# Moving the last two second-stage pieces of one batch two steps ahead in a hand-written schedule

## The chip, the cores and the metric

The kernel runs on one core of one Trainium2 chip. The metric is the time of one execution on the device in microseconds (us). A core has a matrix engine (PE, whose weight loads are listed as PEld), a vector engine (DVE), a scalar engine (ACT), a general engine (POOL) and a queue engine (SP), which run side by side and wait for each other through semaphores. SP and POOL issue the transfers (DMA).

## The reference

The input x has 8 batches of 3008 tokens with 256 channels. Each batch is filtered along the token axis by a Fourier transform, a multiplication with a complex filter and the inverse transform. The result goes, token by token, through a layer pair with a leaky activation whose slope is given per hidden unit:

```python
X = np.fft.rfft(x, axis=1)                  # x: 8 x 3008 x 256
Y = X * (filt_r + 1j * filt_i)[None]
y = np.fft.irfft(Y, n=3008, axis=1).reshape(24064, 256)
h = y @ w_in                                # 256 x 2048
g = np.maximum(h, 0) + alpha * np.minimum(h, 0)
out = g @ w_out                             # 2048 x 256
```

## The kernel before

The transform of 3008 = 47 x 64 points is done in stages of matrix products. For each batch there are four kinds of pieces. Sixteen `piece_a` are the 47-point transform: a matmul (L245) into a psF bank, evicted to `asb` by ACT (L324), saved to `a_dram` and read back turned as `at`. Twelve `piece_b`, numbered by `kp`, are the **second stage**: two matmuls (L265) each and an eviction by ACT (L269) into one of six slots of `uw_s`. Twelve `piece_c` are the first step back (matmuls L292, evicted by ACT to `v`, L324); `turn_c` writes a quarter of `v` to `v_dram` after each third of them (L301), and after the last `load_z` reads it back as `zt` (L310). Sixteen `piece_d` end it (matmuls L317, evictions to `yT`, L324).

Between the second stage and `piece_c` the filter is applied, for two pieces at a time, by `scale`:

```python
if kp % 2:
    late.append((self.scale, (kp, iu - 1)))
...
uu, ww = w[:, 512 * iu : 512 * iu + 1024], w[:, 0:1024]
...
nc.vector.tensor_mul(...[:, 0 : iu // 2 + 1 : iu // 2], uu..., f)     # L278
for o in (0, 64):
    nc.gpsimd.dma_start(out=uu[o : o + 64], in_=ww[64 - o : 128 - o], accum_op=OP.add)   # L281
```

One DVE multiply (L278) makes both products of a pair. One stays in the pair's own slots (`uu`), the other goes to slots 0 and 1 of `uw_s` (`ww`), which all pairs share. Two transfers issued by POOL (L281) then add `ww`, with its halves of the partitions swapped, to `uu`. `piece_c` reads `uu` after that.

The layer pair runs over 47 blocks of 512 tokens, each of 16 steps, so there are 752 steps in all; step 16n + j does row group j of block n. `up` makes the two matmuls of a step (L618) into `hps`; on every second step ACT evicts two row groups to `gtb` (L634), and DVE makes the negative part times slope minus one in `m_s` (two L640; in row group 6 ACT makes it, L638). After every fourth step the sum of the two is owed, and `settle` does it on DVE (L821) in the step that follows. The second layer follows about a block behind, so many matmuls per step, either as plain products (`eight`, L669) or with fewer products of sums (`seven`, L691). Blocks 3 and 4 are of the second kind. Their sums on DVE (L650, L652, L658) are placed by the table `SUMS`: for block 3 from step 65 on. `seven` begins with 16 matmuls over the rows of the block in order, and goes on to the products with the sums in `ss`.

The order of all work is written out by hand. `PLACES` gives, for each batch after the first, the steps of the pieces a, b, c and d. `put` files them, and each step runs in this order: what is in `late` from the step before, the sums, the pieces of this step, `settle`, `up`, and the matmuls of the second layer:

```python
flush()
for b, w, h in ahead.pop(step, ()): ...
    b.sums(w, h)
for fn, args in plan.pop(step, ()):
    fn(*args)
settle()
blk.up(j)
while todo and done < (step - LAG) / 16: ...
```

An engine's instructions stand in the order in which the program writes them. In batch two the second-stage pieces 8 and 9 stand on step 58 and are scaled on step 59; pieces 10 and 11 stand on steps 63 and 64 and are scaled on step 65; the last `piece_c` stand on steps 70 to 72, `turn_c` on 72 and 73, and the first `piece_d` on step 80.

Of the kernel before, what the change touches and what calls it, by code (L numbers as in the profile page):

```python
# [20 lines left out]
NH = 32  # L21
PLACES = (
    ((3, 4, 4, 6, 14, 15, 17, 17, 19, 19, 22, 22, 24, 24, 25, 25),
     (34, 34, 38, 38, 45, 46, 52, 52, 58, 58, 63, 64),
     (48, 50, 55, 55, 55, 60, 66, 70, 71, 71, 72, 72),
     (80, 80, 80, 80, 82, 89, 92, 95, 100, 101, 103, 107, 109, 118, 124, 150)),
    ((-34, -32, -31, -29, -27, -21, -21, -20, -18, -18, -17, -16, -12, -11, -10, -10),
# [857 lines left out]
```

## Time and profile before

| what | value |
|---|---|
| median of 3 runs | 761.42 us |
| the runs | 761.05, 761.42, 762.9 us |
| the profiled execution | 762.9 us |
| its span | 761.1 us |
| granted clock of PE | 0.999 |
| mean DMA rate | 142 GB/s |

The profile is of one execution. Times in its rows count from the start of its span; about 1.8 us of the execution lie around the span. A row of a timeline gives the start, the length from the first start to the last end, the engine, the line, the operation with its tiles, and in brackets how long the engine stood idle before it and what ended that. Lengths of neighbouring rows overlap, since an operation's length takes in its way through the engine; what one costs in a row of them is seen from start to start. Names of tiles stand without their buffer numbers.

### The profile page before, as it was taken

The numbers are of one execution on the slowest core, as the hardware profiler recorded it, in microseconds if no ns is written. First come the engines' busy times: TensorE is split into PE (matmuls) and PEld (weight loads), VectorE is DVE, ScalarE is ACT, GpSimd is POOL, SyncE is SP. The second block draws the span as 40 slices with busy tenths as digits, with TensorE's granted clock in tenths as the row PEclk, the third lists the DMA queues.
The fourth block names the chain that finished last, engine by engine and source line by source line (L and its number), as shares of the span: only waits on it lengthen the run. The fifth ranks groups of instructions, "written<-read, shape, count | busy, mean of one in ns | idle before, by whom it ended". The sixth has DMA issues, their size and how long they took to land.

```text
span 761.1 us, 19855 instructions
## 1 busy us (share of the span) xinstructions
PE 744.2 (98%) x7812; PEld 539.6 (71%) x7812; DVE 694.6 (91%) x1298; ACT 673.8 (89%) x1083; POOL 162.4 (21%) x236
## 2 busy tenths in 40 slices
PE   7989989999999999999999999999999999999998
PEld 5746656776777777776778777777677776777766
DVE  5887877998999998899999999999998998999994
ACT  6898989999999998999899998999989898888873
POOL 9631421132021220232013211221100221010100
PEclk9999999999999999999999999999999999999999
DMA  9995888868975597666876659865586355522122
GB/s 163 192 233 154 146 163 227 181 139 169 197 160 126 110 186 180 139 126 135 192 166 142 134 120 198 184 139 114 106 184 137 74 108 112 140 61 67 43 65 62
DMA packets 100790, 107.97 MB, mean 142 GB/s; under 512 B 10568, under 2 KB 81496, under 8 KB 100696
## 3 DMA queue, kind: packets, MB, share of 16 engines
q1 hardware_dynamic: 80136, 70.05, 35.9%
q0 software_dynamic: 20416, 36.58, 29.9%
q8 instruction: 61, 1.00, 0.6%
q14 instruction: 33, 0.27, 0.1%
q10 hardware_dynamic: 144, 0.07, 0.0%
HBM read 55.41 MB, written 46.66 MB: 134 GB/s over the span
## 4 chain that ended last, share of the span: by engine, by line
PE 90%; DVE 3%; DMA 3%; ACT 1%; issue 1%; SPq 0%; POOL 0%; DVEq 0%; ACTq 0%
PE hps L618 40%; PE op L691 30%; PE op L669 6%; PE psF L245 3%; PE psF L317 3%; PE psF L265 2%; PE psF L292 2%; DMA uw_s<-uw_s 2%; DVE gtb L821 1%; DVE m_s L640 1%; PE op L723 1%; ACT gtb L634 1%; PE hps L364 1%; DVE uw_s L278 1%; DMA zt<-v_dram 1%
## 5 line engine op out<-in xcount | busy, mean ns | idle before, releaser
L618 PE MATMUL hps<-yT,win_s 128*128 128x512 f16 (+3 forms) x1600 | 447.4, 366 | 0.4 <-ACT yT L324 0.4
L634 ACT ACTIVATE gtb<-hps 128x1024 f16<-128x1024 f32 x376 | 386.1, 1028 | 51.3 <-PE hps L618 48.5
L691 PEld LDWEIGHTS <-gtb 128*128 128x128 f16 x3040 | 206.0, 98 | 100.0 <-issue 1.0
L640 DVE TENSOR_SCALAR m_s<-gtb,alm_s 128x512 f16<-128x512 f16 x705 | 215.3, 351 | 35.5 <-ACT gtb L634 34.0
L821 DVE TENSOR_TENSOR gtb<-gtb,m_s 128x2048 f16<-128x2048 f16 x188 | 229.3, 1220 | 5.3 <-ACT m_s L638 3.2
L618 PEld LDWEIGHTS <-win_s 128*128 128x128 f16 x1600 | 135.2, 98 | 25.5 <-issue 3.9
L691 PE MATMUL op<-wout_s,gtb 128*128 128x128 f16 x1824 | 153.2, 219 | 0.0
L281 POOL DMA_DIRECT2D uw_s<-uw_s x84 | 72.3, 1002 | 332.5 <-DVE uw_s L278 207.7
L691 PEld LDWEIGHTS <-ss 128*128 128x128 f16 x1216 | 83.1, 98 | 39.1 <-DVE ss L652 1.6
L691 PE MATMUL op<-tw_s,gtb 128*128 128x128 f16 x1216 | 105.0, 219 | 0.0
L691 PE MATMUL op<-tw_s,ss 128*128 128x128 f16 x1216 | 103.6, 219 | 1.3 <-DVE ss L652 1.3
L669 PE MATMUL op<-wout_s,gtb 128*128 128x256 f16 x512 | 76.9, 272 | 0.3 <-DVE osb L594 0.3
L656 POOL DMA_DIRECT2D gtb<-gtb x28 | 28.0, 998 | 207.5 <-ACT gtb L634 139.1
L669 PEld LDWEIGHTS <-gtb 128*128 128x128 f16 x512 | 50.0, 98 | 31.3
L324 ACT ACTIVATE asb<-psF 96x512 f16<-96x512 f32 x112 | 65.7, 601 | 1.8 <-PE psF L245 0.9
L324 ACT ACTIVATE yT<-psF 128x376 f16<-128x376 f32 x118 | 56.8, 493 | 4.7 <-PE psF L317 3.7
L278 DVE TENSOR_TENSOR uw_s<-uw_s,filt 128x2048 f16<-128x2048 f16 x42 | 51.2, 1220 | 5.7 <-DMA uw_s<-uw_s 4.0
L324 ACT ACTIVATE v<-psF 128x512 f16<-128x512 f32 x88 | 52.0, 603 | 5.1 <-PE psF L292 4.1
L201 POOL DMA_DIRECT2D xs<-in_x_dram x64 | 52.0, 977 | 5.2 <-issue 2.4
L269 ACT ACTIVATE uw_s<-psF 128x512 f16<-128x512 f32 x84 | 50.0, 605 | 2.9 <-PE psF L265 2.0
L652 DVE TENSOR_TENSOR ss<-ss,gtb 128x1024 f16<-128x1024 f16 x76 | 52.0, 685 | 0.1
L650 DVE TENSOR_TENSOR ss<-gtb 128x1024 f16<-128x1024 f16 (+1 forms) x75 | 51.9, 692 | 0.0
(125 smaller groups left out, 643.1 us busy)
## 6 DMA issues: line engine op xcount, KB each, us to landing
out_dram<-osb SPq DMA_DIRECT2D x127, 128.0 KB
xs<-in_x_dram POOLq DMA_DIRECT2D x64, 188.0 KB, 5.5
a_dram<-asb SPq DMA_DIRECT2D x28, 384.0 KB
uw_s<-uw_s POOLq DMA_DIRECT2D x84, 128.0 KB, 3.4
v_dram<-v SPq DMA_DIRECT2D x112, 96.0 KB
zt<-v_dram SPq DMA_DIRECT2D x28, 384.0 KB
at<-a_dram SPq DMA_DIRECT2D x20, 384.0 KB
gtb<-gtb POOLq DMA_DIRECT2D x28, 256.0 KB, 3.8
```

Of the source, the lines that this page charges most:

```text
L201: nc.gpsimd.dma_start(out=xc[(b, c)][h * N1 : h * N1 + N1], in_=xrow(b, h, c))
L278: nc.vector.tensor_mul(w.rearrange("p (i d) -> p i d", d=1024)[:, 0 : iu // 2 + 1 : iu // 2], uu.unsqueeze(1).to_broadcast([128, 2, 1024]), f)
L281: nc.gpsimd.dma_start(out=uu[o : o + 64], in_=ww[64 - o : 128 - o], accum_op=OP.add)
L324: nc.scalar.activation(o, i, AF.Copy)
L618: nc.tensor.matmul(self.hps[:, j % 2, ca:cb], win_s[:, kt, j * 128 : (j + 1) * 128], yT[:, kt, at : at + cb - ca], start=(kt == 0), stop=( ...
L634: nc.scalar.activation(g, hs, AF.Copy)
L640: nc.vector.tensor_scalar(ms[:, i], g[:, i], 0.0, a, OP.min, OP.mult)
L650: nc.vector.tensor_add(z1, a21, a22)
L652: nc.vector.tensor_add(z2, z1, a11)
L669: nc.tensor.matmul(op[:, si % 2], self.pair(k // 2)[:, k % 2, 128 * si : 128 * si + 128], wout_s[:, k], start=(k == 0), stop=(k == 15))
L691: nc.tensor.matmul(acc[:, 128 * i : 128 * i + 128], x[:, k, 128 * i : 128 * i + 128], b[:, k], start=first and k + i == 0, stop=k == 7, sk ...
L821: nc.vector.tensor_add(g, g, ms)
```

## The change

The last two second-stage pieces of batch two, `kp` 10 and 11, stand on steps 61 and 62 instead of 63 and 64.

```diff
 PLACES = (
     ((3, 4, 4, 6, 14, 15, 17, 17, 19, 19, 22, 22, 24, 24, 25, 25),
-     (34, 34, 38, 38, 45, 46, 52, 52, 58, 58, 63, 64),
+     (34, 34, 38, 38, 45, 46, 52, 52, 58, 58, 61, 62),
      (48, 50, 55, 55, 55, 60, 66, 70, 71, 71, 72, 72),
```

Each piece takes its two matmuls and its eviction along. The `scale` of the pair, filed with the second of them, goes from step 65 to step 63 with its two transfers. On PE the four matmuls L265 stand sooner. On ACT the two evictions L269 stand ahead of the hidden-layer evictions of steps 61 and 63. On DVE the multiply L278, which stood behind four L640 and the L821 that settles the last rows of block 3, now stands between the first two and the last two of these L640, ahead of that L821. On POOL and on SP the order of the issues stays as it was.

## The prediction

> **What bounds the kernel now.** I read the page first, then the busy times by stretch, then the chain of waits and the timelines of DVE, PE, ACT and POOL around steps 61 to 73. From the page: the span, the busy times and the shares of the chain.
>
> ```profile
> span 761.1 us, 19855 instructions
> ...
> PE 744.2 (98%) x7812; PEld 539.6 (71%) x7812; DVE 694.6 (91%) x1298; ACT 673.8 (89%) x1083; POOL 162.4 (21%) x236
> ...
> PE 90%; DVE 3%; DMA 3%; ACT 1%; issue 1%; SPq 0%; POOL 0%; DVEq 0%; ACTq 0%
> ...
> ```
>
> PE is busy 98% of the span and carries 90% of the chain, so a microsecond in which PE stands still is a microsecond lost. Where it stands still is seen in the busy times by stretch (PE, PEld, DVE, ACT, POOL, then clock, DMA share, GB/s):
>
> ```profile
> ...
> 84.00:128.00 44.00, 39.95 (x344) 26.91 (x342) 34.46 (x62) 39.85 (x67) 11.11 (x15) 1.00 0.81 182
> 128.00:761.10 633.10, 629.37 (x6756) 459.60 (x6753) 597.55 (x1129) 566.01 (x905) 108.93 (x138) 1.00 0.62 134
> ...
> ```
>
> From 128 us on PE is idle 633.10 - 629.37 = 3.73 us in all, so a delay that exists at 128 us is not won back: there is next to no idle time to take it from. The change sits inside the stretch 84 to 128 us, where PE is idle 4.05 us. In the chain of waits (start, length, what) this is what stands in that stretch:
>
> ```profile
> ...
> 86.37 4.46 DMA uw_s<-uw_s
> ...
> 92.99 4.08 DMA uw_s<-uw_s
> ...
> 99.27 6.00 DMA uw_s<-uw_s
> ...
> 105.35 1.22 DVE uw_s L278
> ...
> 116.89 4.09 DMA zt<-v_dram
> ...
> ```
>
> A multiply of a pair of second-stage pieces (DVE, L278) writes its second half into the one shared block, uw_s slots 0 and 1, from which two POOL-issued transfers (L281) add it to the pair. The next multiply may not write there until these transfers have landed. That is the chain: three landings of 4.46, 4.08 and 6.00 us, each followed by a multiply; the last, of pieces 10 and 11, starts at 105.35. The DVE timeline (start, length, operation, idle time before and what ended it) shows it waiting:
>
> ```profile
> ...
> 98.98 1.22 DVE L821 TENSOR_TENSOR gtb<-gtb,m_s 128x2048 f16<-128x2048 f16 x1
> 100.12 0.61 DVE L640 TENSOR_SCALAR m_s<-gtb,alm_s 128x512 f16<-128x512 f16 x2
> 101.59 0.61 DVE L640 TENSOR_SCALAR m_s<-gtb,alm_s 128x512 f16<-128x512 f16 x2 [0.86 <-ACT gtb L634]
> 102.24 1.23 DVE L821 TENSOR_TENSOR gtb<-gtb,m_s 128x2048 f16<-128x2048 f16 x1
> 105.35 1.22 DVE L278 TENSOR_TENSOR uw_s<-uw_s,filt 128x2048 f16<-128x2048 f16 x1 [1.88 <-DMA uw_s<-uw_s]
> 106.49 0.69 DVE L650 TENSOR_TENSOR ss<-gtb 128x1024 f16<-128x1024 f16 x1
> 107.09 0.70 DVE L640 TENSOR_SCALAR m_s<-gtb,alm_s 128x512 f16<-128x512 f16 x2
> 107.72 0.67 DVE L652 TENSOR_TENSOR ss<-ss,gtb 128x1024 f16<-128x1024 f16 x1
> ...
> 110.04 1.21 DVE L821 TENSOR_TENSOR gtb<-gtb,m_s 128x2048 f16<-128x2048 f16 x1
> ...
> ```
>
> The row at 105.35 is the multiply: DVE had nothing it was allowed to do from 103.47 (102.24 + 1.23) and stood 1.88 us until the transfers of pieces 8 and 9 landed at about 105.3. So the multiply that the change moves is already ready too early, by 1.88 us. The PE timeline of the same time:
>
> ```profile
> ...
> 103.29 0.55 PE L691 MATMUL op<-wout_s,gtb 128*128 128x128 f16 x7
> ...
> 104.33 0.55 PE L691 MATMUL op<-wout_s,gtb 128*128 128x128 f16 x7
> 104.72 0.59 PE L618 MATMUL hps<-yT,win_s 128*128 128x512 f16 x2
> ...
> 108.45 0.34 PE L691 MATMUL op<-tw_s,ss 128*128 128x128 f16 x3 [1.04 <-DVE ss L652]
> 108.62 0.60 PE L292 MATMUL psF<-uw_s,twi_s 128*128 128x256 f16 x4
> ...
> 110.18 0.28 PE L691 MATMUL op<-tw_s,ss 128*128 128x128 f16 x2 [0.24 <-DVE ss L652]
> 110.62 0.60 PE L292 MATMUL psF<-uw_s,twi_s 128*128 128x256 f16 x4 [0.16 <-DMA uw_s<-uw_s]
> ...
> 112.61 0.86 PE L245 MATMUL psF<-xs,wf_s 94*96 94x512 f16 x2 [0.57 <-ACT v L324]
> ...
> 121.03 0.51 PE L317 MATMUL psF<-wi_s,zt 96*128 96x94 f16 x8 [0.33 <-DMA zt<-v_dram]
> 121.94 0.70 PE L317 MATMUL psF<-wi_s,zt 96*128 96x94 f16 x8 [0.41 <-ACT yT L324]
> ...
> 123.21 0.38 PE L618 MATMUL hps<-yT,win_s 128*128 128x512 f16 x1 [0.35 <-ACT yT L324]
> ...
> ```
>
> The row at 108.45 is PE waiting 1.04 us for the sum L652, which stands behind the multiply on DVE. This is today's price of that wait.
>
> **The change part by part.** Pieces 10 and 11 go from steps 63 and 64 to 61 and 62. The multiply is put off to the step after the last piece, so it goes from step 65 to step 63, with its two transfers.
>
> *Matmuls and evictions.* Four matmuls L265 and two evictions L269 change place; none is added. The evictions of now:
>
> ```profile
> ...
> 99.57 0.60 ACT L269 ACTIVATE uw_s<-psF 128x512 f16<-128x512 f32 x1 [0.24 <-PE psF L265]
> ...
> 101.44 0.60 ACT L269 ACTIVATE uw_s<-psF 128x512 f16<-128x512 f32 x1
> ...
> 109.04 1.08 ACT L324 ACTIVATE v<-psF 128x512 f16<-128x512 f32 x2 [1.35 <-PE psF L292]
> 110.02 1.03 ACT L634 ACTIVATE gtb<-hps 128x1024 f16<-128x1024 f32 x1
> 111.35 0.72 ACT L638 ACTIVATE m_s<-gtb,alm_s 128x512 f16<-128x512 f16 x1 [0.31 <-DVE gtb L821]
> 111.98 1.07 ACT L324 ACTIVATE v<-psF 128x512 f16<-128x512 f32 x2
> ...
> ```
>
> They start at 99.57 and 101.44 and would come up to two steps sooner. PE could wait once for a bank that an eviction frees, at most the length of one, 0.60 us, about step 63; I take 0 to 0.6 and count nothing, because PE then runs into the stall below, which ends at a time that this does not move. Without that stall it would cost up to 0.6.
>
> *The multiply on DVE.* In the program order of DVE the multiply passes two L640 (step 63) and one L821 (step 64). Before, these three were done at 101.59 to 103.47, in the shadow of the transfer. After, the multiply stands at their head from about 100.7 (100.12 + 0.61) and waits for the same landing, because pieces 8 and 9 and their transfers are not moved. So it still starts at 105.35; its wait grows from 1.88 to about 4.6 us, and the two L640, the L821 and all sums are queued behind it. From start to start the rows give 1.14 for a multiply (106.49 - 105.35), 0.60 for an L650 (107.09 - 106.49), 0.63 for two L640 (107.72 - 107.09) and 1.14 for an L821 (100.12 - 98.98). The L821 then starts at 105.35 + 1.14 + 0.63 = 107.12 and is done 1.22 later, at 108.34, instead of 103.47.
>
> That order decides this is shown only by the row at 105.35, behind which the L650 waited until 106.49. [...]
>
> *Who waits for that L821.* It finishes rows 12 to 15 of block 3. PE reads them with the 13th of the 16 products of seven's first product (L691). Seven of these run from 103.29 and seven from 104.33, 0.056 us apart (104.72 - 104.33 = 0.39 for seven), so the 13th is due at 104.33 + 5 x 0.056 = 104.61. PE takes up work 0.06 after DVE's end (108.45 against 107.72 + 0.67). It resumes at 108.40: a new stall of 3.79 us.
>
> *What is given back.* The wait of 1.04 at 108.45 goes: the first L652 would start at 107.12 + 1.14 + 0.60 + 0.63 = 109.49 and end at 110.16, while PE wants it at 108.45 - 1.04 + 3.79 = 111.20. So the four L292 of pieces 8 and 9, now at 108.62, come 3.79 - 1.04 = 2.75 later, at 111.37. The second L652 no longer holds PE either (0.24 at 110.18), nor the transfer of pieces 10 and 11 (0.16 at 110.62). That transfer's issue is as early as now, and the two behind it on POOL with it, since they follow the multiply's end:
>
> ```profile
> ...
> 106.87 1.66 POOL L281 DMA_DIRECT2D uw_s<-uw_s  x2 [6.32 <-DVE uw_s L278]
> ...
> ```
>
> What is late next is ACT. After the four L292 it has two v evictions, an L634, an L638 and two more v evictions, the first of which frees the bank for PE's L245 at 112.61. Measured from the L292 at 108.62: v at +0.42, L634 at +1.40, its end at +2.43, so L638 could start at 111.05. It starts at 111.35, held by DVE's L821 (110.04 + 1.21). After: L634 at 112.77, L638 at 113.80; the L821, displaced by 0.63 + 1.14 = 1.77, ends at 113.02 and holds nothing. So L638 comes 113.80 - 111.35 = 2.45 later, the v evictions at 111.98 and the L245 at 112.61 too. That is the sum up to there: **+2.45 us**. PE, which now takes 112.61 - 0.57 - 108.62 = 3.42 to this L245, 0.40 of it waits that go, arrives at 111.37 + 3.02 = 114.39 and waits 0.67 for ACT.
>
> *The way on.* The v evictions start the writes of v and the loads of zt (the chain's 4.09 at 116.89), for which PE waits 0.33, then 0.41 and 0.35 for yT. All of it is released by what is 2.45 late, so these waits stay and the delay goes on to 128 us, after which nothing absorbs it. The earlier pieces buy nothing: their results are held by the landing either way.
>
> The sum against the profiled execution: 762.9 us, of which 761.1 is span and 1.8 lies around it, goes to 765.35. The median of the three runs, 761.42, is 1.48 below that execution; the same 2.45 on it gives **763.9 us**, 0.32% slower. A measurement of this kernel can tell about 0.3%, here 2.28 us, from no change, so the forecast lies just beyond that.
>
> Bounds of the unknown: if what is given back is not given back, because something else is late in its place, the cost is the whole new stall, 3.79 (765.2). From below, it hangs on the landing:
>
> ```profile
> ...
> DMA to landing us min/median/max: 2.7/3.5/6.0
> ```
>
> ```profile
> ...
> uw_s<-uw_s POOLq DMA_DIRECT2D x84, 128.0 KB, 3.4
> ...
> ```
>
> If it comes e sooner than here in both kernels, the stall is 3.79 - e and the wait that goes is 1.04 - e, but not below 0. I take the landing as it is in this trace; for one up to about 1 us sooner the cost stays near 2.5.
>
> **The rivals.** *A sooner landing in ordinary runs of both.* At 4.08, the chain's shortest, e is 1.92 and the cost 1.87 (763.3); at the page's median of 3.4, e is 2.60 and the cost 1.19 (762.6). For it: the landings at 86.37 and 92.99 were both under 4.5. Against it: this pair competes with writes of v and of the output, and DVE's stall at 105.35 ends the chain. All of it is within 0.3%. Chance 0.23. [...]
>
> *Not slower: a sooner landing in the changed kernel alone.* The place is the same transfer. Were it 2.45 faster there, because the moved evictions shift the a_dram write next to it, the cost would be nil, so the point is a landing in 3.5 us. At 2.7, the shortest in the view above, the stall is 3.79 - 3.3 = 0.49, less than the 1.04 + 0.31 that go: 0.9 faster (760.5). Over 0.3% faster needs a landing in 1.3 us, or waits further on to go too (0.33, 0.41, 0.35). Against it: neither its issue nor the writes of v ahead of it move. Chance 0.10, half of it over 0.3%.
>
> *Absorbed on the way to yT.* If v and zt move faster for being later, the 0.33 + 0.41 + 0.35 = 1.09 can go: 2.45 - 1.09 = 1.36, 762.8. For it: the stretch 84 to 128 has DMA busy 0.81 and the loads on POOL would be out of the way. Against it: the latter two waits are between PE and ACT. Chance 0.05.
>
> **How the numbers follow.** The forecast has 0.62; of it 0.05 falls under 2.28 us. Slower by over 0.3%: 0.57. Within: 0.05 + 0.23 + 0.05 + 0.05 = 0.38. Faster: 0.05. The likeliest case alone has 763.5 to 765.2. The range takes in the sooner landing down to 0.2 of cost, 761.6, and the whole stall, 765.2; it leaves out the case that isn't slower and little more.
>
> **What would show it.** In the changed profile: the multiply's row on DVE near 105.3 with an idle time before it of about 4.6 instead of 1.88, followed by two L640 and an L821 that ends near 108.3; one PE wait of about 3.8 at an L691 from gtb, put down to L821; no wait for L652; the L245 row near 115.1; PE's busy time from 130 us on the same. The forecast is wrong if the multiply waits under 3.5, if PE's new wait is under 2.5, or if a second wait on ACT or zt grows beside it.

## The result and the profile after

| | before | after |
|---|---|---|
| median of 20 runs each | 762.34 us | 764.38 us |
| span of the profiled execution | 761.1 us | 764.4 us |
| time of the profiled execution | 762.9 us | 766.22 us |

The ratio is 1.003 with a 95% interval of 1.0019 to 1.0041: the change is slower, by about 2.3 us. Lines of the page of the changed kernel:

```profile
span 764.4 us, 19855 instructions
...
PE 745.8 (98%) x7812; PEld 540.6 (71%) x7812; DVE 694.1 (91%) x1298; ACT 673.9 (88%) x1083; POOL 162.7 (21%) x236
...
PE 87%; DMA 5%; DVE 3%; ACT 2%; POOL 2%; issue 1%; DVEq 0%; POOLq 0%; ACTq 0%
...
```

The span is 3.3 us longer. PE's share of the chain went from 90 to 87%. The DVE timeline of the changed kernel at the place of the change (start, length, operation, idle time before and what ended it):

```profile
...
100.07 0.61 DVE L640 TENSOR_SCALAR m_s<-gtb,alm_s 128x512 f16<-128x512 f16 x2
104.94 1.23 DVE L278 TENSOR_TENSOR uw_s<-uw_s,filt 128x2048 f16<-128x2048 f16 x1 [4.26 <-DMA uw_s<-uw_s]
106.08 0.61 DVE L640 TENSOR_SCALAR m_s<-gtb,alm_s 128x512 f16<-128x512 f16 x2
106.73 1.23 DVE L821 TENSOR_TENSOR gtb<-gtb,m_s 128x2048 f16<-128x2048 f16 x1
107.87 0.68 DVE L650 TENSOR_TENSOR ss<-gtb 128x1024 f16<-128x1024 f16 x1
...
109.00 0.68 DVE L652 TENSOR_TENSOR ss<-ss,gtb 128x1024 f16<-128x1024 f16 x1
...
```

The multiply of pieces 10 and 11 now stands behind the two L640 at 100.07 and waits 4.26 us for the landing (1.88 before). The two L640 and the L821 that stood ahead of it now follow it, and the L821 ends at 106.73 + 1.23 = 107.96 instead of 103.47. The PE timeline:

```profile
...
104.62 0.44 PE L691 MATMUL op<-wout_s,gtb 128*128 128x128 f16 x5
108.01 0.40 PE L691 MATMUL op<-wout_s,gtb 128*128 128x128 f16 x2 [2.95 <-DVE gtb L821]
108.20 1.06 PE L618 MATMUL hps<-yT,win_s 128*128 128x512 f16 x2
109.05 0.95 PE L691 MATMUL op<-wout_s,gtb 128*128 128x128 f16 x7
...
112.37 0.60 PE L292 MATMUL psF<-uw_s,twi_s 128*128 128x256 f16 x4
...
116.08 0.86 PE L245 MATMUL psF<-xs,wf_s 94*96 94x512 f16 x2 [0.95 <-ACT v L324]
...
125.27 0.70 PE L317 MATMUL psF<-wi_s,zt 96*128 96x94 f16 x8 [0.76 <-ACT yT L324]
...
```

After five products (L691) PE stops, for 2.95 us and put down to that L821. The wait for L652 of before is gone. What was not expected is the length of the rows behind it: two L618 at 108.20 take 1.06 us and seven L691 at 109.05 take 0.95, where the same forms took 0.59 and 0.55. The busy times by stretch (PE, PEld, DVE, ACT, POOL, then the granted clock of PE, DMA share, GB/s) say why:

```profile
...
104.90:108.00 3.10, 0.16 (x3) 0.00 (x0) 3.03 (x5) 1.24 (x2) 1.54 (x3) 0.97 0.42 110
108.00:111.40 3.40, 3.39 (x21) 2.29 (x22) 3.40 (x9) 0.89 (x2) 1.19 (x3) 0.52 0.89 125
111.40:113.00 1.60, 1.60 (x18) 1.21 (x16) 1.60 (x5) 1.22 (x3) 0.00 (x0) 1.00 0.64 123
128.00:764.40 636.40, 632.70 (x6787) 461.77 (x6784) 599.75 (x1134) 569.34 (x911) 110.31 (x139) 1.00 0.63 134
...
```

For about 3.4 us after the stall the granted clock is half (0.52). To tell the stall from the half clock, runs are also sorted below by their mean granted clock: a run with some 3.4 us at half clock has a mean of 0.997 or 0.998 (a low clock, in what follows; 0.997 in both traced runs of the change, 0.998 in the two other traced runs with such a stretch; the sorting takes every such run for one with a stretch of this kind, which only the traced runs show). In the three comparisons behind the experiments the kernel before had 5 such runs of 84, and its other runs a median of 761.83, 761.61 and 761.92 us. The last row shows that from 128 us on PE is idle 636.40 - 632.70 = 3.70 us (3.73 before): the delay is carried to the end. What comes between, on ACT:

```profile
...
113.77 1.03 ACT L634 ACTIVATE gtb<-hps 128x1024 f16<-128x1024 f32 x1
114.83 0.72 ACT L638 ACTIVATE m_s<-gtb,alm_s 128x512 f16<-128x512 f16 x1
115.45 1.06 ACT L324 ACTIVATE v<-psF 128x512 f16<-128x512 f32 x2
...
```

L638 starts at 114.83 right after its L634, so the L821 on DVE no longer holds it, as forecast.

### The profile page after: what moved, and what is told of

Same layout as the page of the kernel before. It is cut to its first block, busy times and chain, and to the rows that moved or that the text cites. A ratio compares the mean times of both kernels' runs of the same rounds, so it can differ in the third digit from the quotient of the medians.

```text
span 764.4 us, 19855 instructions
## 1 busy us (share of the span) xinstructions
PE 745.8 (98%) x7812; PEld 540.6 (71%) x7812; DVE 694.1 (91%) x1298; ACT 673.9 (88%) x1083; POOL 162.7 (21%) x236
## 4 chain that ended last, share of the span: by engine, by line
PE 87%; DMA 5%; DVE 3%; ACT 2%; POOL 2%; issue 1%; DVEq 0%; POOLq 0%; ACTq 0%
PE hps L618 40%; PE op L691 31%; PE op L669 5%; PE psF L245 3%; PE psF L317 3%; DMA uw_s<-uw_s 2%; PE psF L292 2%; PE psF L265 2%; DMA filt<-in_filt_i_dram 2%; ACT gtb L634 1%; DVE uw_s L278 1%; DVE gtb L821 1%; PE op L723 1%; DVE m_s L640 1%; POOL xs L201 1%
## 5 line engine op out<-in xcount | busy, mean ns | idle before, releaser
L618 PE MATMUL hps<-yT,win_s 128*128 128x512 f16 (+3 forms) x1600 | 448.4, 367 | 0.4 <-ACT yT L324 0.4
L634 ACT ACTIVATE gtb<-hps 128x1024 f16<-128x1024 f32 x376 | 386.0, 1028 | 52.0 <-PE hps L618 49.2
L691 PEld LDWEIGHTS <-gtb 128*128 128x128 f16 x3040 | 206.8, 98 | 103.8 <-DVE gtb L821 3.1
L640 DVE TENSOR_SCALAR m_s<-gtb,alm_s 128x512 f16<-128x512 f16 x705 | 213.9, 347 | 36.7 <-ACT gtb L634 35.3
L821 DVE TENSOR_TENSOR gtb<-gtb,m_s 128x2048 f16<-128x2048 f16 x188 | 228.6, 1216 | 5.3 <-ACT m_s L638 3.2
L691 PE MATMUL op<-wout_s,gtb 128*128 128x128 f16 x1824 | 154.2, 220 | 3.0 <-DVE gtb L821 3.0
L618 PEld LDWEIGHTS <-win_s 128*128 128x128 f16 x1600 | 135.4, 98 | 25.5 <-issue 3.9
L691 PEld LDWEIGHTS <-ss 128*128 128x128 f16 x1216 | 83.1, 98 | 37.4
L691 PE MATMUL op<-tw_s,gtb 128*128 128x128 f16 x1216 | 105.0, 219 | 0.0
L691 PE MATMUL op<-tw_s,ss 128*128 128x128 f16 x1216 | 103.4, 219 | 0.0
L278 DVE TENSOR_TENSOR uw_s<-uw_s,filt 128x2048 f16<-128x2048 f16 x42 | 51.1, 1217 | 8.2 <-DMA uw_s<-uw_s 7.6
L269 ACT ACTIVATE uw_s<-psF 128x512 f16<-128x512 f32 x84 | 50.0, 604 | 2.7 <-PE psF L265 1.7
L652 DVE TENSOR_TENSOR ss<-ss,gtb 128x1024 f16<-128x1024 f16 x76 | 51.8, 682 | 0.1
```

Source lines behind the costliest of these rows:

```text
L278: nc.vector.tensor_mul(w.rearrange("p (i d) -> p i d", d=1024)[:, 0 : iu // 2 + 1 : iu // 2], uu.unsqueeze(1).to_broadcast([128, 2, 1024]), f)
L618: nc.tensor.matmul(self.hps[:, j % 2, ca:cb], win_s[:, kt, j * 128 : (j + 1) * 128], yT[:, kt, at : at + cb - ca], start=(kt == 0), stop=( ...
L634: nc.scalar.activation(g, hs, AF.Copy)
L640: nc.vector.tensor_scalar(ms[:, i], g[:, i], 0.0, a, OP.min, OP.mult)
L652: nc.vector.tensor_add(z2, z1, a11)
L691: nc.tensor.matmul(acc[:, 128 * i : 128 * i + 128], x[:, k, 128 * i : 128 * i + 128], b[:, k], start=first and k + i == 0, stop=k == 7, sk ...
```

## The experiments

All comparisons are with the kernel before, run beside each kernel on the same chip.

**The change again.** No edit.

> The change itself, unaltered, beside the other runs on one chip. By the first comparison 1.9 to 4.1 us over before. Runs with a mean clock of 0.999 or more at 1.4 to 2.2 over before, by a landing that in ordinary runs comes up to about 2 us sooner than in the first profile; runs with 0.997 or 0.998 (6 of 20 at first) some 2 us above those.

Measured: 764.99 against 761.97 us, ratio 1.0033 (1.0019 to 1.0046). Four of 12 runs have the low clock, at 766.17 to 766.61; the other eight have a median of 764.07, 2.15 above the 761.92 of before. With the first comparison, 10 of 32 runs have the low clock. Its profile again has a stall at L821 (2.9 us) and a clock of 0.50 behind it. Both profiles of the change are of runs with the low clock (766.22 and 766.61 us), so no trace shows the change without it.

**The pieces sooner, the multiply where it was.**

```diff
-            if kp % 2:
+            if self.b == 1 and kp == 11:
+                put(64, late.append, (self.scale, (kp, iu - 1)))
+            elif kp % 2:
                 late.append((self.scale, (kp, iu - 1)))
```

> Pieces 10 and 11 on steps 61 and 62 as in the change, but their multiply and its two transfers stay on step 65. If the order on DVE is the whole cost, this runs as the kernel before: within 0.1% (0.8 us) of it, the multiply near 105 with about 1.9 us of idle time before it, PE waiting about 1 us for L652 and not for L821. The rival, that the moved matmuls and evictions cost the time (a bank not free, evictions pushed back), has it 2 us slower than before, like the change.

Measured: 762.25 against 761.85 us, ratio 1.0006 (0.9989 to 1.0023). The DVE timeline of this kernel:

```profile
...
102.13 1.23 DVE L823 TENSOR_TENSOR gtb<-gtb,m_s 128x2048 f16<-128x2048 f16 x1
103.54 1.23 DVE L280 TENSOR_TENSOR uw_s<-uw_s,filt 128x2048 f16<-128x2048 f16 x1 [0.18 <-DMA uw_s<-uw_s]
104.68 0.68 DVE L652 TENSOR_TENSOR ss<-gtb 128x1024 f16<-128x1024 f16 x1
...
```

The multiply stands behind the L821 again. The moved matmuls and evictions alone cost nothing clear of noise; it is the moved multiply. Three of 12 runs have the low clock, one of them at 767.62; the other nine have a median of 761.98, 0.15 over the 761.83 of before, where the change had 2.15. So the low clock does not hang on the moved multiply alone. In this execution the landing came at about 103.5, nearly 2 us sooner than in the trace of before, and DVE waited 0.18 us only, not the 1.9 expected, and PE did not wait for L652 at all: how soon the transfers land differs from run to run. PE waited 1.43 us at an L292 for the transfers of pieces 10 and 11 instead.

**The multiply further up or down DVE's order.** In the first kernel pieces 10 and 11 stand on steps 62 and 63, so that only the L821 is displaced; in the second both stand on step 60, so that two more L640 are.

```diff
-     (34, 34, 38, 38, 45, 46, 52, 52, 58, 58, 61, 62),
+     (34, 34, 38, 38, 45, 46, 52, 52, 58, 58, 62, 63),   # multiply on step 64
+     (34, 34, 38, 38, 45, 46, 52, 52, 58, 58, 60, 60),   # multiply on step 61
```

> Pieces on steps 62 and 63, so the multiply stands on step 64: behind the four L640, ahead only of the L821 of the last rows of block 3. By the order on DVE, the L821 ends 0.63 us sooner than in the change, at about 107.3 to 107.7, the new PE stall is 2.4 to 3.1 us and the whole is 1.2 to 2.0 us over before, clearly nearer to the change than to before. If instead the cost comes by degrees with how far the pieces are moved, it lies halfway, at +1.0. If the half clock after the stall needs a stall of about 3 us, it shows here more seldom than in the change.

> Pieces on step 60, both, so the multiply stands on step 61, ahead of four L640 and the L821 (the change: two L640 and the L821). By the order on DVE the L821 ends 0.63 us later than in the change, the stall of PE grows by 0.6 and the time by 0.4 to 0.9 over the change, 2.4 to 3.5 over before. If the half clock comes from PE standing idle for about 3 us, it is seen here in more runs than the 6 of 20 of the change (mean granted clock 0.997 to 0.998). If the cost does not follow the order on DVE, the time is that of the change.

Measured: 763.83 against 761.85 us, ratio 1.0022 (1.0008 to 1.0036), and 764.32 against 761.67, ratio 1.0031 (1.0021 to 1.0042). DVE with the multiply on step 64, then with it on step 61:

```profile
...
104.50 1.23 DVE L278 TENSOR_TENSOR uw_s<-uw_s,filt 128x2048 f16<-128x2048 f16 x1 [1.72 <-PE op L691]
105.64 1.22 DVE L821 TENSOR_TENSOR gtb<-gtb,m_s 128x2048 f16<-128x2048 f16 x1
...
```

```profile
...
104.21 1.23 DVE L278 TENSOR_TENSOR uw_s<-uw_s,filt 128x2048 f16<-128x2048 f16 x1 [3.73 <-DMA uw_s<-uw_s]
105.35 1.14 DVE L640 TENSOR_SCALAR m_s<-gtb,alm_s 128x512 f16<-128x512 f16 x4
106.52 1.23 DVE L821 TENSOR_TENSOR gtb<-gtb,m_s 128x2048 f16<-128x2048 f16 x1
...
```

From the multiply's start to the end of the L821 it is 2.36 us here (105.64 + 1.22 - 104.50), 3.02 in the change (106.73 + 1.23 - 104.94) and 3.54 with two L640 more (106.52 + 1.23 - 104.21): the displaced instructions, one after the other. The runs without the low clock follow: their medians lie 763.29 - 761.83 = 1.46 us over before with the multiply on step 64, 764.07 - 761.92 = 2.15 in the change, and 764.32 - 761.61 = 2.71 with it on step 61. The intervals of the ratios overlap, so the times alone would not show the order. What was expected of PE did not come. Its waits (total us, times, longest) with the multiply on step 64, then on step 61:

```profile
...
PE op L691 <- DVE gtb L821: 1.5, 1, 1.5
...
```

```profile
...
PE op L691 <- DVE gtb L821: 1.2, 1, 1.2
PE psF L265 <- ACT v L324: 0.9, 1, 0.9
...
```

The stalls are shorter than the 2.95 of the change, where 2.4 to 3.1 and more than in the change were expected: both multiplies started sooner (104.50 and 104.21 against 104.94), and in the second kernel PE had already waited 0.9 us for a bank at a moved L265, so its time is not the order on DVE alone. (The wait of the multiply on step 64 is put down to an L691 of PE, not to the landing, so its start does not time that landing.) The low clock did not follow: 4 of 12 runs with the multiply on step 64, but none of 9 with it on step 61, where I expected more; with a stall of 1.2 us in the one traced, that is no test of a longer stall.

**An own block, so that no landing is waited for.** The second product of this one pair goes elsewhere; the multiply becomes two of half the size.

```diff
+            if self.b == 1 and kp == 11:
+                ww = ss.rearrange("p a k c -> p (a k c)")[:, 3072:4096]
+                nc.vector.tensor_mul(ww, uu, f[:, 0])
+                nc.vector.tensor_mul(uu, uu, f[:, 1])
+            else:
                 nc.vector.tensor_mul(...)
```

> The change, but the second product of pieces 10 and 11 goes to a part of ss that is free then, instead of the shared slots 0 and 1, so that the multiply (made as two of half the size) needs no landing. If the landing of the transfers of pieces 8 and 9 is what holds DVE, the multiply starts near 100.8 with no idle time, PE has no wait for L821 nor for L652, and the kernel is faster than before by 1 to 2 us (the waits of 1.04, 0.24, 0.16 and 0.57 go), so 3 to 4 us faster than the change. If the stall came from elsewhere, it stays at about 3 us and the time at that of the change.

Measured: 762.04 against 761.85 us, ratio 1.0002 (0.9989 to 1.0015): the loss of the change is gone, the expected gain over before is not there. On DVE:

```profile
...
103.61 0.69 DVE L280 TENSOR_TENSOR ss<-uw_s,filt 128x1024 f16<-128x1024 f16 x1
...
112.33 0.69 DVE L657 TENSOR_TENSOR ss<-ss,gtb 128x1024 f16<-128x1024 f16 x1 [2.59 <-DMA uw_s<-ss]
...
```

The multiply waits for nothing, but the second L652 (line 657 here) waits 2.59 us for the transfers that read ss, and PE 1.21 us for it. (The profiled execution is the slowest of the twelve, 765.65 us, with a mean clock of 1.0; it was already some 3 us late at the multiply of pieces 8 and 9, at 100.16 against 97.19 before, so it shows the wait but not what the median lost.) So the next kernel puts the block into an osb buffer (`ww = p_osb.tile([128, 1024], FP16, name="osb")`), and another one does the same with the pieces on steps 63 and 64.

> As the kernel with an own block for pieces 10 and 11, but the block is a fourth osb buffer instead of a part of ss, so that no sum on DVE waits for its transfers (2.6 us there). If the landing alone set the cost, neither the multiply nor a sum waits, PE waits for neither L821 nor L652, and the time is 0.5 to 2 us below the kernel before. If it comes out as the kernel before again, what is gained on DVE is taken back by the transfers of pieces 10 and 11, which then travel together with those of 8 and 9: PE waits at L292 or for zt instead.

> The kernel before, pieces 10 and 11 on steps 63 and 64, with the own block in an osb buffer for this pair. Its multiply stands behind the L821 and waits for no landing, so that DVE's 1.88 us before the multiply go. If the landing is the only difference that the change brought out, this and the change with the own block are alike (within 0.5 us of each other): with the landing out of the way it doesn't matter on which step the pieces stand. If sooner pieces are worth something in themselves, this is slower than the change with the own block by over 0.8 us.

Measured: the change with this block 761.56 against 761.67 us, ratio 0.9995 (0.9987 to 1.0004); the kernel before with it 762.13 against 761.97, ratio 1.0003 (0.999 to 1.0016). DVE of the first:

```profile
...
100.22 0.68 DVE L280 TENSOR_TENSOR osb<-uw_s,filt 128x1024 f16<-128x1024 f16 x1
101.00 0.69 DVE L281 TENSOR_TENSOR uw_s<-uw_s,filt 128x1024 f16<-128x1024 f16 x1
...
102.26 1.23 DVE L826 TENSOR_TENSOR gtb<-gtb,m_s 128x2048 f16<-128x2048 f16 x1
...
```

No wait before the half multiplies at 100.22 and 101.00, and the L821 starts at 102.26 as before the change. With the landing out of the way the two places of the pieces can't be told apart (0.9995 and 1.0003, with overlapping intervals), and the change loses nothing that can be seen: its cost is the landing in front of DVE's queue. The expected gain over before is not had, though. What PE still waits for in this stretch (total us, times, longest), first the sooner pieces, then the old places:

```profile
...
PE psF L245 <- ACT v L329: 0.9, 1, 0.9
PE psF L297 <- ACT v L329: 0.5, 1, 0.5
...
```

```profile
...
PE psF L297 <- DMA uw_s<-osb: 1.3, 1, 1.3
...
```

With the old places the transfers of pieces 10 and 11 land late for PE (1.3 us); with the sooner ones it is ACT that is late (0.9 us at L245). That pointed to one more edit: the last five piece_c a step sooner, on 69, 70, 70, 71, 71.

> The change with the own block in an osb buffer, and the last five piece_c a step sooner (69, 70, 70, 71, 71 for 70, 71, 71, 72, 72), which the sooner transfers of pieces 10 and 11 allow. The two v evictions of pieces 10 and 11 then stand ahead of the L634 and L638 of step 71, so the wait of 0.9 us of PE at L245 goes or halves: 0.3 to 1 us faster than the same without it, 0.5 to 1.3 us under before. If the transfers have not landed by step 71, PE waits there and nothing is gained.

Measured: 761.24 against 761.97 us, ratio 0.9989 (0.9978 to 1.0000), none of 12 runs with the low clock. Its PE waits:

```profile
...
PE psF L297 <- ACT v L329: 0.5, 1, 0.5
PE psF L245 <- ACT asb L329: 0.5, 2, 0.3
...
```

The 0.9 us for v are gone, two waits of 0.5 in all for asb came (0.2 before). It has the lowest median of this study, at the edge of what can be told from before, and its interval overlaps that of the same kernel with piece_c on the old steps. That sooner pieces can be used for a gain is suggested by this, not shown.

**The multiply behind the first sums.** Pieces on 61 and 62, and `put(66, self.scale, kp, iu - 1)` instead of `late`, so that the multiply follows the first L652.

> Pieces on steps 61 and 62, but the multiply put off to step 66, behind the first L652 of block 3. On DVE nothing urgent is then behind the multiply: no wait of PE for L821 or for L652 (0 against 3.0 in the change and 1.0 before). Its two transfers come up to 1.2 us later than before, and PE then waits for them at the four L292 of pieces 10 and 11, about 1 us. By the order on DVE the whole is 1.5 to 2.5 us faster than the change and within 0.6 us of the kernel before, on either side. If the move of the pieces themselves cost the time, it is as slow as the change.

Measured: 765.54 against 761.67 us, ratio 1.0042 (1.0026 to 1.0058): by its median slower than the change, though the intervals overlap, and against all expectation. PE of this kernel:

```profile
...
110.70 0.60 PE L294 MATMUL psF<-uw_s,twi_s 128*128 128x256 f16 x4 [1.71 <-ACT m_s L640]
...
121.93 0.51 PE L319 MATMUL psF<-wi_s,zt 96*128 96x94 f16 x8 [2.08 <-DMA zt<-v_dram]
...
123.49 1.36 PE L620 MATMUL hps<-yT,win_s 128*128 128x512 f16 x2
...
```

No wait for L821 or L652, and the first rows of PE run ahead of before; but PE loses it all again at L292 and then 2.08 us at the first piece_d, for zt. The queue of SP, this kernel and then the kernel before, shows that zt is asked for at the same time:

```profile
...
116.89 1.26 SPq L312 DMA_DIRECT2D zt<-v_dram  x3
...
```

```profile
...
116.89 1.26 SPq L310 DMA_DIRECT2D zt<-v_dram  x3
...
```

So the multiply has two sides. Behind it stand the sums; ahead of it stands a path of its own, from the landing over the multiply, its transfers, piece_c and v to zt, which is as late as in the kernel before whatever DVE does in between. I had priced one wait at L292 and left out that path. It explains that nothing was gained. In this trace the loss is two other things: zt, asked for at the same time, came 0.90 us later (first piece_d at 121.93, 121.03 before), for a reason that stays open, and behind the wait came the half clock. Five of 6 runs have the low clock; the sixth took 763.43, still 1.82 over the 761.61 of before. The stretches:

```profile
...
119.80:122.90 3.10, 0.62 (x12) 0.46 (x11) 2.34 (x4) 1.32 (x3) 0.00 (x0) 0.97 0.99 280
122.90:126.10 3.20, 3.06 (x19) 1.85 (x19) 1.93 (x3) 1.13 (x3) 0.94 (x1) 0.50 1.04 376
...
```

**Filling the stall.** The change with matmuls into a bank that nobody reads, just before the 13th product of block 3, so that PE isn't idle: 48, then 20.

```diff
+                        if self.n == 3 and self.sent == 12:
+                            warm(48, bank())
                         nc.tensor.matmul(acc...
```

> The change, with 48 matmuls more, of 128 columns, into a bank that nobody reads, placed just before the product at which PE stalls: some 2.6 us of work that fills the wait of 3 us. DVE, ACT and the landing are as in the change. If the half clock after the stall (PEclk 0.50 from 108 to 111 in the trace of the change) comes from PE standing idle, the clock stays at 1.00 here in every run, and the kernel is 0.5 to 1.5 us faster than the change, though it has more work, and its slow tail of runs near 766 is gone. If the half clock is not tied to the idle time, it is as slow as the change or slower.

> The change with 20 matmuls more of 128 columns before the stalling product, 1.1 us of work, which fits into the stall also where it is short (48 of them were 1.3 us more than the stall in the profiled execution). If idle time of PE brings the half clock, runs with a mean clock of 0.997 or 0.998 get rarer than 6 in 20, and the time is 0 to 0.8 us below the change (1.2 to 2.3 over before). If they are as frequent, the half clock is not tied to the length of this stall, and the time is that of the change.

Measured: 765.61 against 761.85 us with 48, ratio 1.0047 (1.0026 to 1.0068), and 765.97 against 761.67 with 20, ratio 1.0043 (1.0027 to 1.006). Both are no faster than the change, and low clocks are as frequent, 3 of 8 and 4 of 10. PE with 48, then with 20:

```profile
...
104.51 2.84 PE L459 MATMUL psF<-idx_s 128*128 128x128 f16 x48
107.19 0.28 PE L693 MATMUL op<-wout_s,gtb 128*128 128x128 f16 x2
...
```

```profile
...
104.75 1.28 PE L459 MATMUL psF<-idx_s 128*128 128x128 f16 x20
107.76 0.28 PE L693 MATMUL op<-wout_s,gtb 128*128 128x128 f16 x2 [1.73 <-DVE gtb L823]
...
123.76 0.51 PE L317 MATMUL psF<-wi_s,zt 96*128 96x94 f16 x8 [1.39 <-DMA zt<-v_dram]
...
```

With 48 the filling ended at 107.19, while the L821 had ended at 105.84: the landing had come sooner, and the filling was itself the delay. With 20 the clock stayed full at the stall (1.00 from 104 to 116 us), but the half clock (0.53) then came at the next thin place, where PE waits for zt and yT:

```profile
...
122.40:125.40 3.00, 1.19 (x17) 0.98 (x18) 2.33 (x4) 1.86 (x4) 0.00 (x0) 0.94 1.00 249
125.40:128.70 3.30, 3.15 (x21) 1.84 (x19) 1.94 (x3) 0.99 (x3) 0.94 (x1) 0.53 1.05 371
...
```

The experiment doesn't tell what the half clock costs, since the filling moved the delay. With the change it does show that the half clock came at two places of this stretch: behind the stall (0.52, the change) and behind the first rows of piece_d (0.53, 20 matmuls more).

## Why the prediction was right

The forecast was 763.9 us, or 2.45 more than before; measured were 2.04 between the medians, and ratios of 1.003 and 1.0033, about 2.3 and 2.5 us. Step by step against the first profile:

| step of the prediction | forecast | profile after |
|---|---|---|
| multiply starts, after a wait of | 105.35, 4.6 us | 104.94, 4.26 us |
| L821 of the last rows ends | 108.34 | 107.96 |
| new stall of PE at the 13th product | 3.79 us | 2.95 us |
| wait for L652 | gone | gone |
| four L292 of pieces 8 and 9 | 111.37 | 112.37 |
| L638, held by ACT and not by DVE | 113.80 | 114.83 |
| L245, wait of PE before it | 115.06, 0.67 us | 116.08, 0.95 us |
| delay at the L245 | 2.45 us | 3.47 us |
| delay of the span | 2.45 us | 3.3 us |

The mechanism is the one forecast, and the kernels with the multiply alone left, displaced by other amounts, or freed from the landing show it: the cost is gone when the multiply stays, and gone when it need not wait. Its sizes were off, in opposite directions.

*The stall.* It was 0.84 shorter than forecast. Of that about 0.4 is the landing (104.94 against 105.35, and the L821's end at 107.96 against 108.34), and about 0.3 that PE came later: its five products started at 104.62, so the 13th was due at 104.90 and not at 104.61. The rest is counting: the prediction counts from when the 13th is due, the row only from the end of the product before it, at 105.06. PE's coming later fits the wait for a bank that the prediction bounded at 0 to 0.60 and counted as absorbed, and it was absorbed. The landing is what the first rival was about, and it is half right: the landing was seen up to 2.5 us sooner (102.84, last section), so the stall differs from run to run. The measured cost of 2.04 lies between the rival's 1.87 and the forecast's 2.45. The lower end of the range, 0.2 of cost, takes by the sum 3.79 - e a landing in about 2.4 us (6.00 - 3.59), which no run shows: the shortest landing of these transfers is 2.6 us in the traces of before and after, and the one in question took 6.00 and 5.64 us.

*The wait given back.* The prediction took 1.04 us for the wait for L652, which is the idle time from the end of the row before. Counted as it counted the stall, it is more, as this PE row of before shows:

```profile
...
107.02 0.39 PE L691 MATMUL op<-wout_s,gtb 128*128 128x128 f16 x4
...
```

The products are 0.056 us apart, so the next was due at 107.02 + 4 x 0.056 = 107.24. It came at 108.45, 1.21 us late: 0.17 more was given back than the sum has.

*The clock.* The prediction took every PE row behind the stall at its old length. From the resumption at 108.01 to the L292 at 112.37 it is 4.36 us; before, the same work took 108.62 - 104.61 - 1.21 = 2.80, without the wait for L652. The 1.56 more is the term that is missing from the sum. At the L292 the forecast delay of 2.75 becomes 2.75 - 0.39 (resumption at 108.01, not 108.40) - 0.17 + 1.56 = 3.75, which is the measured one (112.37 - 108.62); without the half clock it would have been 2.19. By the mean clock it comes in 10 of 32 runs. Those lie some 2.3 us over the others, more than the 1.56 at its place; what makes the rest is open. So the median comes out near the forecast because runs without the low clock lie somewhat below it (2.15 us above before, where 2.45 was forecast) and the others well above; part of the closeness is luck. In the time itself it is so too: the forecast stood on a median of 761.42 from three runs, and 20 runs gave 762.34, so 764.38 lies 0.48 over 763.9 although the cost is 0.41 under 2.45.

One of the prediction's own signs of being wrong showed in part: a second wait on ACT grew beside the stall, at the L245 to 0.95 us (0.57 before, 0.67 forecast) and for yT to 0.76 (0.41 before).

The case that isn't slower did not show: no profile of the change has a landing soon enough to leave the L821 where it was. Nor was anything won back on the way to yT: the wait of 0.33 for zt went, but the one for yT at 125.27 grew by 0.35.

## What to carry to other kernels

On an engine that works in order, as DVE did in these traces, an instruction that waits for a transfer holds up everything behind it: in the change the multiply waited 4.26 us, and the two L640 behind it started at 106.08, though the L634 that makes what they read had ended on ACT at 101.81. Moving its producer up can pull it past ready work that others wait for, and that work then waits too. Before moving it either way, follow both sides: what is queued behind it, and the path that it feeds, since taking one wait away (the multiply behind the sums) may only show the other (there 2.08 us for zt). Where the wait is for a shared block, a second block makes the place matter less: here it took the loss of the change away (ratio 0.9995 to the kernel before), but won nothing clear of noise over the kernel before.

## What the runs showed of the hardware

After three thin stretches PE's granted clock fell to about half: to 0.52 over 3.40 us in the change, 0.50 over 3.20 us in the kernel with the multiply behind the sums, and 0.53 over 3.30 us in the one with 20 matmuls more. In the stretches PE had been busy 0.16 of 3.10, 0.62 of 3.10 and 1.19 of 3.00 us, with longest waits of 2.95, 2.08 and 1.39 us. By the mean clock it did not come in every run of these kernels: in 10 of 32, 5 of 6 and 4 of 10. It did not follow the wait of 1.04 us in the kernel before, nor waits of 1.71 us (at the L292, multiply behind the sums) and 1.73 us (at the L691, 20 matmuls more), behind which the clock stayed at 1.00. So the longest wait alone does not tell where it comes: it followed one of 1.39 us and not these two. What sets it off, and why only some runs have it, these runs do not show.

The landing of the transfers of pieces 8 and 9, by the start of the multiply of pieces 10 and 11 that waits for it, came between 102.84 and 105.23 in the five profiles with pieces 10 and 11 on steps 61 and 62 and that multiply put down to the landing (the change twice, the two fillings, the pieces alone). The multiply of pieces 8 and 9, which these transfers follow, started between 96.22 and 97.30. From the one start to the other it is 6.62 us at the least and 7.93 at the most (8.16 in the trace of before): one profile prices such a landing to no better than 1.5 us.
